# Sliding-window attention followed by a squared-ReLU MLP: six x tiles, margins on DMA landings, biases of the first blocks by TensorE, and the second block's loads on SyncE's queue

## The chip, the cores and the metric

One core of one Trainium2 chip. The metric is device time in microseconds (us) of that core, median over executions; one of them is taken with the hardware profiler. The profiled span is from the first to the last instruction and is 1.7 to 1.8 us shorter than the time that is measured from outside (before: 314.6 against 312.9).

## The reference, cut to what matters

```python
# q, k, v: [8 batches, 8 heads, 576 tokens, 64], float32
scores = scale * q @ k.T                      # per batch and head
rel    = pos[:, None] - pos[None, :]
mask   = (rel >= 0) & (rel < 128)             # window of 128 tokens
scores = where(mask, scores - slopes[h] * abs(rel), -1e9)
attn   = softmax(scores) @ v
x      = attn, heads side by side             # [4608 tokens, 512]
h      = x @ w_in                             # [4608, 2048]
out    = (maximum(h, 0) ** 2) @ w_out         # [4608, 512], float32
```

## The kernel before

The whole program is laid out by a list scheduler at build time: every piece of work is a task with engines, a cost, dependencies and buffers, and the plan is emitted in the order of its estimated starts. Each engine then works through its list in order and waits on semaphores. Some 60 hand-tuned adjustments (`ADJ`) shift single tasks.

The parts that matter here are the order of the first loads, the number of blocks whose keys and queries are loaded by the hardware queues (`N_HW`; the others are cast and loaded by GpSimd), and the buffers:

```python
FIRST = ["b0", "b1", "b2", "i0", "i1", "o0", "b3", "i2", "i3", "o1", "o2", "o3", "b4", "b5", "b6", "b7"]
N_HW = 1                 # b = block of 128 tokens (k, q, v), i = quarter of w_in, o = quarter of w_out
SIZE = {"kq": 4, "v": 9, "kqT": 7, "P": 3, "x": 3}
...
        if split:        # m < N_HW: float32 pieces into a stage, by SyncE and ScalarE, then a cast on chip
            stage = stages[m]
            ...
                        e.dma_start(view(stage, i)[:, r], source(src, m, split)[:, :, r])
        else:            # one cast-in-flight load each for keys and queries, by GpSimd
                    nc.gpsimd.dma_start(view(kq[s_kq[m].idx], i), source(src, m, split))
```

A block's keys and queries are transposed (by TensorE for the first eight blocks, by DMA transposes on SyncE's queue after them), 64-row matmuls give the scores, ScalarE the exponentials, and a product with a precomputed mask on VectorE brings in window and bias:

```python
                nc.scalar.activation(flat(Pt[sP.idx]), sS[i].tile..., AF.Exp, bias=0.0, scale=scale)
                ...
                    nc.vector.tensor_tensor(flat(Pt[sP.idx]), flat(Pt[sP.idx]), flat(masks), op=ALU.mult)
```

In the profile, `tp` are transposes of keys and queries, `s` scores, `P` probabilities, `pv` products with values, `x` the normalized attention, `xp` and `xT` its transposes, `h` products with w_in, `rt` their rectification, `g` the squares, `o` products with w_out.

The softmax here doesn't subtract the row's maximum and nothing guards it: scores larger than these inputs give would overflow.

Of the kernel before, what the change touches and what calls it, by code (L numbers as in the profile page):

```python
# [15 lines left out]
FIRST = ["b0", "b1", "b2", "i0", "i1", "o0", "b3", "i2", "i3", "o1", "o2", "o3", "b4", "b5", "b6", "b7"]  # L16
DIAG = [[0], [1], [2], [3], [4, 5], [6, 7]]
N_HW = 1
N_PE = 8
N_CUT = 1  # L20
N_PVH = 0
N_WARM = 8
FILL = 0.7
LEAD = 720
# [3 lines left out]
UNITS = {0: [(0, 128, 4), (128, 128, 4), (256, 128, 4), (384, 128, 4)], 1: [(0, 256, 2), (256, 256, 2)],  # L28
         2: [(0, 256, 2), (256, 256, 2)]}
PIECES = [4, 4, 4, 4]  # L30
CUT = 384
SIZE = {"kq": 4, "v": 9, "kqT": 7, "P": 3, "x": 3}
# [3 lines left out]
    "e1.2": 99737.5, "e14.1": 197.91, "e16.2": -128.81, "e19.2": -8999803.95, "e2.3": -401.4, "e20.1": 2.03,  # L36
    "e3.1": 99809.35, "e6.3": 99108.3, "fc3.1": -547.61, "fc3.2": -237.14, "fc3.3": -684.14, "fc3.5": -652.43,
    "fc3.7": -100007.3, "fc3.8": -9000379.3, "m18.2": 165.47, "m18.3": -239.22, "n1.1": 100203.0, "n10.1": 495.17,
    "n12.1": 587.74, "n15.0": 308.11, "n16.0": 356.11, "n16.1": 706.81, "n9.0": 332.79, "o0.2.0": -103.48,
    "o0.2.1": -122.14, "o0.2.2": -99562.6, "o1.0.1": -100260.7, "o1.0.2": -100228.4, "o1.1.1": -99628.0,  # L40
    "o1.1.2": -152.7, "o1.1.3": -198.1, "o1.3.1": -99940.7, "o2.0.1": -99143.6, "o2.1.1": 200, "o2.2.0": -615.0,
    "oe1.0.0": -220.3, "ones2": 99179.7, "pv11.1": -99297.74, "pv19.0": -100068.55, "r18.0": 267.47, "r3.1": 99545.79,
    "relufc3.1": -100188.3, "relufc3.5": -99571.3, "reluu0.0.2": -99848.1, "reluu0.1.0": -100044.0,
    "reluu1.1.4": -579.61, "reluu2.0.5": -282.54, "squ0.0.0": -100027.7, "squ1.1.3": -388.31, "squ2.1.1": 40,
    "u0.2.0": -8999828.5, "u0.2.1": -99868.0, "u1.1.0": 39, "u1.1.1": -99305.4, "u1.1.4": -99991.3,
    "u1.1.6": -99367.7, "u2.0.5": -99873.0, "u2.0.6": -468.21, "u2.0.7": -99687.4, "u2.1.1": -187.45,
    "u2.1.2": -482.59, "u2.1.3": 39, "u2.1.7": -266.7,
# [3 lines left out]
class Task:  # L51
# [3 lines left out]
                 "ready", "start", "end", "eng", "seq", "lat", "dma", "name", "count", "gap")  # L55

    def __init__(self, engs, key, emit, deps=(), acq=(), rel=(), lat=None, dma=None, name="", count=1):
        self.engs, self.key, self.emit = engs, key, emit
        self.deps = [d for d in deps if d is not None]
        self.acq, self.rel, self.lat = list(acq), list(rel), lat  # L60
        self.dma, self.name, self.count = dma, name, count
        self.users, self.ready, self.start, self.end, self.eng, self.gap = [], 0.0, None, None, None, 0.0
# [9 lines left out]
class Plan:  # L72


    LAT = {"PE": 210.0, "ACT": 60.0, "DVE": 80.0, "POOL": 200.0, "SP": 200.0, "ACTQ": 200.0}
    BEGIN = {"POOL": 840.0, "SP": 740.0, "ACTQ": 740.0, "ACT": 2550.0, "DVE": 860.0, "PE": 1190.0}
# [4 lines left out]
    NEAR = {"PE": 25, "ACT": 60, "DVE": 25}  # L81
# [17 lines left out]
    def order(self):  # L99
# [16 lines left out]
        def avail(t):  # L116
            at = t.ready
            if t.dma is not None:
                lane = self.lanes["SW" if "POOL" in t.engs else "HW"]
                if len(lane) >= self.LANES:  # L120
                    at = max(at, lane[-self.LANES])
# [15 lines left out]
        while len(done) < n_all:  # L137
# [40 lines left out]
            for u in t.users:  # L178
                left[u] -= 1
                at = st + dur if u.engs.keys() == {e} and t.dma is None else t.end  # L180
                if "SP" in u.engs and t.dma is None:
                    at += self.TO_SP
                u.ready = max(u.ready, at)
# [9 lines left out]
def kernel(  # L193
# [44 lines left out]
    masks = const.tile([128, H, 2, 128], BF16)  # L238
    dist = const.tile([128, 2, 128], FP32)
# [35 lines left out]
    def act(n):  # L275
        return n * 0.95 + 115.0

    def dve(n, rate=1):
        return n / rate / 0.96 + 180.0

    def dve_p(n, rate=1):
        return n / rate / 0.96 + 185.0
# [31 lines left out]
    t_ident = plan.add({"DVE": 230.0}, EARLY + 1, build_ident, [t_iota], name="ident")  # L314
# [7 lines left out]
    for part in (1, 0):  # L322
        key = EARLY + 2 if part else -1e5 + 1100
        t_dist[part] = plan.add({"DVE": 430.0}, key, lambda part=part: build_dist(part), [t_ident],
                                name=f"dist{part}", later=0.0 if part else 18000.0)
        for p in range(H):
# [3 lines left out]
            t_mask[part].append(plan.add({"ACT": act(128)}, key + 1 + p, build_mask, [t_dist[part]], name=f"mask{part}.{p}"))  # L330

    def ones(ts):
        for t in ts:
            nc.vector.memset(t[:, :, D:D + 1], 1.0)
    t_ones = [plan.add({"DVE": 320.0}, EARLY + 3, lambda: ones(tiles["v0"][0:2]), name="ones0"),
              plan.add({"DVE": 900.0}, -1e5 + 300, lambda: ones(tiles["v0"][2:]), name="ones1", later=11000.0),
              plan.add({"DVE": 1200.0}, -1e5 + 900, lambda: ones(tiles["v"]), name="ones2", later=20000.0)]
# [4 lines left out]
    def zero():  # L342
        for m in halves:
            if m - B < size["v"]:
                nc.vector.memset(tiles["v"][m - B][64:128, :, 0:D], 0.0)
            if m - B < size["kqT"]:
                nc.vector.memset(tiles["kqT"][m - B][:, 0:C, 64:128], 0.0)
    t_zero = plan.add({"DVE": 1300.0}, -1e5 + 950, zero, name="zero", later=25000.0)


# [29 lines left out]
    def load_block(m, key):  # L380
# [10 lines left out]
        if split:  # L391
            stage = stages[m]
            t_l = []
            for i, src in enumerate((k, q)):
                for r, (eng, e) in enumerate((("SP", nc.sync), ("SP", nc.sync) if m else ("ACTQ", nc.scalar))):
                    def fetch(i=i, src=src, r=r, e=e):
                        e.dma_start(view(stage, i)[:, r], source(src, m, split)[:, :, r])
                    t_l.append(plan.add({eng: 740.0}, key + 0.1 * i, fetch, dma=330.0, lat=700.0 if i else 1650.0,
# [7 lines left out]
            engs = {"DVE": 480.0, "ACT": 600.0} if m else {"DVE": 480.0}  # L406
# [4 lines left out]
        else:  # L411
            def fetch_kq():
                for i, src in enumerate((k, q)):
                    nc.gpsimd.dma_start(view(kq[s_kq[m].idx], i), source(src, m, split))  # L414
            t_kq[m] = [plan.add({"POOL": 1780.0}, key, fetch_kq, [], [s_kq[m]], dma=2 * ns,
                                name=f"lkq{m}", count=2)]

        def fetch_v():
            nc.gpsimd.dma_start(tile_of(s_v[m])[0:n, :, 0:D], source(v, m))  # L419
        l_v = plan.add({"POOL": 890.0}, key + 0.2, fetch_v, [t_zero] if kb == HALF else [], [s_v[m]],  # L420
                       dma=ns, name=f"lv{m}")
        t_v[m] = [l_v, t_ones[0 if m < 2 else 1 if m < B else 2]]
# [26 lines left out]
    def transpose_kq(m, due):  # L449
# [4 lines left out]
        if m >= N_PE:  # L454
            def flip():
                nc.sync.dma_start_transpose(out=tile_of(sT)[:, :, 0:n], in_=kq[s_kq[m].idx][0:n, :])
            t_f = plan.add({"SP": 1500.0}, due - 60, flip, t_kq[m] + [t_zero if kb == HALF else None], [sT],
                           [s_kq[m]], dma=1700.0 * n / 128, name=f"kqT{m}")
            t_kqT[m] = [[t_f], [t_f]]
            return  # L460
        t_tp, evs = [None, None], [[], []]
        for i in range(2):
# [13 lines left out]
            pieces = [(0, C // 2), (C // 2, C)] if i and m == 0 else [(0, C)]  # L476
            for c0, c1 in pieces:
                def evac(i=i, st=st, c0=c0, c1=c1, e=len(evs[i])):
# [4 lines left out]
                    else:  # L483
# [4 lines left out]
                                       [t_tp[i]] + evs[i], [], [st], name=f"ev{m}.{i}.{c0}"))  # L488
        last["tp"] = t_tp[1]
        t_kqT[m] = [[evs[0][0], evs[1][0]], evs[0] + evs[1]]  # L490

    def job(j, kind, ms, due):
        nb = len(ms)
        n = 64 if kind == "half" else 128
        for m in ms:
            transpose_kq(m, due)
        before = {m: at[seq[m][0], seq[m][1] - 1] for m in ms if kind != "diag"}
# [15 lines left out]
        bursts = [[0], [1]] if j == 0 else [[0, 1]]  # L513
        for z, grps in enumerate(bursts):
# [15 lines left out]
            for m in set(ms) | set(before.values()):  # L530
                deps += t_kqT[m][0] if z == 0 and len(bursts) > 1 else t_kqT[m][1]
# [11 lines left out]
        for i in range(4):  # L543
# [12 lines left out]
            def mask(w=w, flat=flat):  # L556
                if kind == "full" or (kind == "diag" and nb == 1):
# [13 lines left out]

    def values(j, kind, i, m, nb, sP, t_P, mb, due):
# [4 lines left out]
        if kind == "full":  # L577
            parts = [(slice(0, 128), mb), (slice(128, 256), m)]
# [250 lines left out]
```

## Time and profile before

| | before |
|---|---|
| time, median of 4 runs | 314.64 us (314.49 to 315.82) |
| profiled span, granted TensorE clock | 312.9 us, 1.00 |
| first product with weights / first output product | 15.18 / 20.26 us |
| last store issued / landed / end of span | 310.24 / 311.81 / 312.90 us |

(When the prediction was made three runs were known, with a median of 314.77.)

The chain that ended last, followed back from the end (page of before, share of the span by engine):

```profile
PE 78%; DMA 16%; POOL 3%; issue 1%; ACT 0%; POOLq 0%; SPq 0%
```

and the same chain in order of time for the first 45 us (start us, us, what):

```profile
6.82 0.85 POOL vf L419
7.67 7.46 DMA w_in_sb<-in_moe_w_in_dram
15.14 0.28 issue
15.42 14.97 DMA w_out_sb<-in_moe_w_out_dram
30.39 0.28 issue
30.68 9.89 DMA vf<-in_v_dram
```

Up to 40 us nothing but DMAs of the GpSimd queue stands in it.

### The profile page before, as it was taken

The numbers are of one execution on the slowest core, as the hardware profiler recorded it, in microseconds if no ns is written. First come the engines' busy times: TensorE is split into PE (matmuls) and PEld (weight loads), VectorE is DVE, ScalarE is ACT, GpSimd is POOL, SyncE is SP. The second block draws the span as 40 slices with busy tenths as digits, with TensorE's granted clock in tenths as the row PEclk, the third lists the DMA queues.
The fourth block names the chain that finished last, engine by engine and source line by source line (L and its number), as shares of the span: only waits on it lengthen the run. The fifth ranks groups of instructions, "written<-read, shape, count | busy, mean of one in ns | idle before, by whom it ended". The sixth has DMA issues, their size and how long they took to land.

```text
span 312.9 us, 7112 instructions
## 1 busy us (share of the span) xinstructions
PE 302.9 (97%) x2777; PEld 175.3 (56%) x2820; DVE 171.1 (55%) x492; ACT 173.2 (55%) x336; POOL 105.6 (34%) x131
## 2 busy tenths in 40 slices
PE   6899999999999999999999999999999999999996
PEld 3779757677766744455545554545454444444443
DVE  3757366667666656776666657666656222222211
ACT  4766567657677535855766554676564443444400
POOL 8844597272623855401937203700000000000000
DMA  9999999999999999997999939991220100010022
GB/s 130 184 192 204 172 176 183 144 153 147 206 133 190 198 158 192 145 124 137 152 183 173 180 60 130 197 175 52 51 69 17 69 34 35 37 34 34 34 96 74
DMA packets 165714, 39.54 MB, mean 126 GB/s; under 512 B 156336, under 2 KB 161200, under 8 KB 165680
## 3 DMA queue, kind: packets, MB, share of 16 engines
q0 software_dynamic: 114656, 18.10, 83.8%
q1 hardware_dynamic: 50592, 20.65, 35.8%
q8 instruction: 22, 0.36, 0.4%
q10 hardware_dynamic: 432, 0.33, 0.4%
q14 instruction: 12, 0.10, 0.1%
HBM read 36.70 MB, written 9.44 MB: 147 GB/s over the span
## 4 chain that ended last, share of the span: by engine, by line
PE 78%; DMA 16%; POOL 3%; issue 1%; ACT 0%; POOLq 0%; SPq 0%
PE o L762 34%; PE h L735 27%; PE h L718 7%; PE pv L593 5%; PE s L526 5%; DMA w_out_sb<-in_moe_w_out_dram 5%; DMA kqT<-kq 3%; DMA vf<-in_v_dram 3%; DMA kq<-in_q_dram 3%; DMA w_in_sb<-in_moe_w_in_dram 2%; POOL kq L414 2%; POOL vf L419 1%; POOL vt L419 0%; POOL dist L305 0%; ACT osb L291 0%
## 5 line engine op out<-in xcount | busy, mean ns | idle before, releaser
L762 PE MATMUL o<-w_out_sb,g 128*128 128x512 bf16 (+2 forms) x565 | 138.4, 373 | 1.9 <-DMA w_out_sb<-in_moe_w_out_dram 0.3
L683 ACT ACTIVATE rt<-h 128x512 bf16<-128x512 f32 x144 | 85.5, 606 | 92.0 <-PE h L735 64.1
L692 DVE TENSOR_TENSOR g<-rt 128x512 bf16<-128x512 bf16 x144 | 59.9, 422 | 74.0 <-ACT rt L683 73.3
L735 PE MATMUL h<-xT,w_in_sb 128*128 128x512 bf16 x368 | 95.1, 379 | 0.8
L762 PEld LDWEIGHTS <-g 128*128 128x128 bf16 x592 | 54.1, 98 | 56.0 <-issue 0.4
L550 ACT ACTIVATE P<-s 128x512 bf16<-128x512 f32 (+1 forms) x136 | 67.3, 581 | 18.1 <-PE s L526 18.1
L735 PEld LDWEIGHTS <-w_in_sb 128*128 128x128 bf16 x384 | 35.3, 98 | 39.5
L558 DVE TENSOR_TENSOR P<-P,masks 128x512 bf16<-128x512 bf16 (+1 forms) x112 | 44.4, 404 | 15.7 <-ACT P L550 11.2
L718 PE MATMUL h<-xT,w_in_sb 128*128 128x128 bf16 (+1 forms) x512 | 46.7, 246 | 1.3 <-DMA w_in_sb<-in_moe_w_in_dram 1.3
L414 POOL DMA_DIRECT2D kq<-in_k_dram x39 | 33.4, 857 | 40.3 <-DMA kqT<-kq 32.5
L718 PEld LDWEIGHTS <-w_in_sb 128*128 128x128 bf16 x512 | 38.4, 98 | 6.6 <-DMA w_in_sb<-in_moe_w_in_dram 1.6
L419 POOL DMA_DIRECT2D vt<-in_v_dram x32 | 27.0, 847 | 43.6 <-PE pv L593 35.4
L615 DVE TENSOR_TENSOR x<-pv,rec 128x256 bf16<-128x256 f32 (+1 forms) x80 | 33.4, 421 | 3.9 <-DMA xT<-x 1.5
L414 POOL DMA_DIRECT2D kq<-in_q_dram x39 | 33.6, 861 | 4.6 <-PE h L718 1.6
L593 PEld LDWEIGHTS <-P 128*128 128x128 bf16 (+1 forms) x576 | 25.1, 101 | 13.0 <-DVE x L615 1.3
L291 ACT ACTIVATE osb<-o 128x512 f32<-128x512 f32 (+1 forms) x23 | 13.6, 592 | 21.0 <-PE o L762 20.8
L611 DVE RECIPROCAL rec<-pv 128x4 f32<-128x4 f32 (+1 forms) x80 | 14.0, 178 | 18.7 <-PE pv L593 17.0
L593 PE MATMUL pv<-vt,P 128*128 128x65 bf16 (+1 forms) x448 | 23.8, 194 | 0.0
L526 PEld LDWEIGHTS <-kqT 64*128 64x128 bf16 x448 | 12.4, 94 | 8.1 <-issue 7.4
L289 DVE COPY osb<-o 128x512 f32<-128x512 f32 (+1 forms) x14 | 9.5, 682 | 13.2 <-PE o L762 12.6
L526 PE MATMUL s<-kqT 64*128 64x128 bf16 (+1 forms) x256 | 15.6, 210 | 0.0
L526 PE MATMUL s<-kqT,kqT 64*128 64x128 bf16 (+1 forms) x192 | 11.4, 209 | 0.2 <-DMA kqT<-kq 0.2
(41 smaller groups left out, 98.2 us busy)
## 6 DMA issues: line engine op xcount, KB each, us to landing
out_dram<-osb SPq DMA_DIRECT2D x31, 256.0 KB, 3.6
kq<-in_k_dram POOLq DMA_DIRECT2D x31, 128.0 KB, 7.1
kq<-in_q_dram POOLq DMA_DIRECT2D x31, 128.0 KB, 7.3
vt<-in_v_dram POOLq DMA_DIRECT2D x24, 128.0 KB, 8.2
w_in_sb<-in_moe_w_in_dram POOLq DMA_DIRECT2D x4, 512.0 KB, 11.1
w_out_sb<-in_moe_w_out_dram POOLq DMA_DIRECT2D x4, 512.0 KB, 15.0
vf<-in_v_dram POOLq DMA_DIRECT2D x8, 128.0 KB, 6.6
out_dram<-osb SPq DMA_DIRECT2D x8, 128.0 KB, 2.3
```

The lines of the kernel that those rows point to most:

```text
L414: nc.gpsimd.dma_start(view(kq[s_kq[m].idx], i), source(src, m, split))
L419: nc.gpsimd.dma_start(tile_of(s_v[m])[0:n, :, 0:D], source(v, m))
L526: nc.tensor.matmul(sS[2 * g2 + r].tile[:, jj * 256 + c0:jj * 256 + c0 + w], tile_of(s_kqT[mk])[rows, c, :], tile_of(s_kqT[mq])[rows, C + c ...
L550: nc.scalar.activation(flat(Pt[sP.idx]), sS[i].tile.rearrange("p (j t) -> p j t", j=2)[:, :, lo:hi], AF.Exp, bias=0.0, scale=scale)
L558: nc.vector.tensor_tensor(flat(Pt[sP.idx]), flat(Pt[sP.idx]), flat(masks), op=ALU.mult)
L593: nc.tensor.matmul(sv.tile[0:n, hi * (D + 1):(hi + 1) * (D + 1)], Pt[sP.idx][:, place(h)].rearrange("p t q -> p (t q)")[:, w], tile_of(s_v ...
L615: nc.vector.tensor_tensor(xt[sx.idx][0:n, hf * 256:(hf + 1) * 256].rearrange("p (h e) -> p h e", h=4), heads(sv)[0:n, :, 0:D], sr.tile[0:n ...
L683: nc.scalar.activation(srt.tile[:, 0:n], slot.tile[:, 0:n], AF.Relu, bias=0.0, scale=1.0)
L692: nc.vector.tensor_tensor(o, i, i, op=ALU.mult)
L718: nc.tensor.matmul(slot.tile[:, f * w:(f + 1) * w], w_in_sb[:, cc, fc * 128:(fc + 1) * 128], xT[:, cc, lo:lo + w], start=cc == 0, stop=cc ...
L735: nc.tensor.matmul(slot.tile, w_in_sb[:, cc, fc * 128:(fc + 1) * 128], xT[:, cc, g * 512:(g + 1) * 512], start=cc == 0, stop=cc == C - 1)
L762: nc.tensor.matmul(slot.tile[:, 0:hi - lo], gt[:, fc, t * 128:(t + 1) * 128], w_out_sb[:, fc, lo:hi], start=fc == 0, stop=fc == FCB - 1)
```

## The change

Its intent: start the products with weights sooner by taking the second block's keys and queries off the GpSimd queue; take the masks of the four first blocks off VectorE by letting TensorE add the bias to the scores; and let the plan assume later DMA landings than estimated (`SLACK`, in ns), with more x tiles to allow for it, so that TensorE's list in the middle of the run does not meet a transfer that is still under way. The core of the diff (the new adjustments, new cost estimates of single instructions and bookkeeping are cut; cut too is that the exponentials which build the masks, no longer needed by the first four blocks, are planned after 14 us):

```diff
-FIRST = ["b0", "b1", "b2", "i0", "i1", "o0", "b3", "i2", "i3", "o1", "o2", "o3", "b4", "b5", "b6", "b7"]
+FIRST = ["b0", "b1", "b2", "i0", "i1", "o0", "b3", "i2", "o1", "o2", "i3", "b4", "o3", "b5", "b6", "b7"]
-N_HW = 1
+N_HW = 2
+SLACK = {"kq": 0.0, "kqT": 5000.0, "v": 4000.0, "x": 2000.0}
-LEAD = 720
+LEAD = 320
-SIZE = {"kq": 4, "v": 9, "kqT": 7, "P": 3, "x": 3}
+SIZE = {"kq": 4, "v": 8, "kqT": 7, "P": 3, "x": 6}
...
+                at += t.slack
                 u.ready = max(u.ready, at)
...
+    def lone(j, m, due):
+        sS = [Slot("a") for _ in range(2)]
+        def biases():
+            for r in range(2):
+                nc.tensor.matmul(bank(sS[r], f"s{r}"), ident,
+                                 slopes[:, 4 * r:4 * r + 4].rearrange("p c q -> p (c q)"), start=True, stop=False)
...
+                    nc.tensor.matmul(sS[r].tile[:, c * 128:(c + 1) * 128], tile_of(s_kqT[m])[rows, c, :],
+                                     tile_of(s_kqT[m])[rows, C + c, :], start=False, stop=c == C - 1)
...
+                nc.scalar.activation(lone_P(sP)[:, r * 512:(r + 1) * 512], sS[r].tile, AF.Exp, bias=0.0, scale=scale)
```

## The prediction

> **What bounds the kernel now.** I read the page first, then the chain of waits, then TensorE's own timeline, then four-microsecond windows of the start, and last each DMA's issue and landing in the trace.
>
> ```profile
> span 312.9 us, 7112 instructions
> PE 302.9 (97%) x2777; PEld 175.3 (56%) x2820; DVE 171.1 (55%) x492; ACT 173.2 (55%) x336; POOL 105.6 (34%) x131
> ...
> PE   6899999999999999999999999999999999999996
> ...
> DMA  9999999999999999997999939991220100010022
> ```
>
> TensorE is full from the third slice (16 us) to the last; VectorE and ScalarE are just over half busy. Matmul busy time hides pipelining, so I also counted. The built program has 2820 matmuls. At the start-to-start pitch that full runs show (215 ns for 512 columns, 109 for 256, 55 for 128, 29 for 65, and 28 for each of a pair of 64-row score matmuls) they need 290.0 us, 5.9 of it warm-up and filler products that compute nothing. Real work is 284.1 us, and 312.9 - 284.1 = 28.8 us are lost. By start-to-start times, run by run, about 14.3 lie before 20.3 us (5.9 filler, 8.4 waiting), about 11.3 between 20.3 and 305, and 3.2 after the last matmul has started (evacuation and store).
>
> The 11.3 are almost no waiting: each of the 32 bursts of 64-row score matmuls costs about 0.10 us on entry and 0.12 on leaving (7 us together), and the rest is 0.01 to 0.04 at each change of operand. The change keeps these bursts. So only the first 20 us can give anything.
>
> ```profile
> 4.71 0.39 PE L270 MATMUL tp<-warm 128*128 128x128 bf16 x4
> 6.39 0.40 PE L470 MATMUL tp<-ident,kq 128*128 128x128 bf16 x4 [1.29 <-DVE kq L289]
> ...
> 13.96 0.28 PE L593 MATMUL pv<-vf,P 128*128 128x65 bf16 x4 [0.28 <-ACT P L550]
> 15.18 1.07 PE L718 MATMUL h<-xT,w_in_sb 128*128 128x128 bf16 x16 [0.94 <-DMA w_in_sb<-in_moe_w_in_dram]
> ...
> 17.76 1.96 PE L718 MATMUL h<-xT,w_in_sb 128*128 128x128 bf16 x32 [0.39 <-DMA w_in_sb<-in_moe_w_in_dram]
> ...
> 20.26 1.02 PE L762 MATMUL o<-w_out_sb,g 128*128 128x512 bf16 x3 [0.32 <-DMA w_out_sb<-in_moe_w_out_dram]
> ```
>
> These are lines of TensorE's timeline (start, duration, what, idle before it and who ended it). The reader should see that the first product with weights (15.18), the next (17.76) and the first output product (20.26) start as their weights land: 15.14, 17.71, 20.22 in the trace. From there the DMA stream, in order on the GpSimd queue, stays just ahead of TensorE: a block's keys and queries land at 38.90 and 39.73, and that block's transposes run here:
>
> ```profile
> 38.00 1.89 PE L762 MATMUL o<-w_out_sb,g 128*128 128x512 bf16 x8
> 39.72 0.61 PE L470 MATMUL tp<-ident,kq 128*128 128x128 bf16 x8
> ```
>
> No idle time stands before it, but there is no room either. That is why TensorE cannot simply run two microseconds further ahead.
>
> **What the Trainium skill says.** (1) "TensorE: Matmul & The Clock Gate", section "Wait — 56ns, not 53.3ns?": warm matmuls start N / 2.4 GHz + about 2.5 ns apart, cold ones N / 1.2 GHz. The trace agrees: 16 products of 128 columns take 0.90 us, the first eight warm-up products start 427 ns apart. (2) "DMA: Bandwidth & Descriptors", section "Issuing engines are not separate DMA queues": DMAs from all issuers share 16 engines, and a second issuer saves only issue time. The trace of before fits: while ScalarE's and SyncE's loads still run, the GpSimd queue moves 421 packets in the fifth microsecond, against some 1200 per microsecond afterwards. (3) The same page, section "Specifications": below 512 B a transfer is off line rate. Keys, queries and values come in 256 B pieces, a 128 KB load takes 0.84 us of the stream, while a 512 KB load of weights takes 2.55. (4) "PSUM — Partial Sum Buffer", section "The four PSUM rules": a matmul without the first-flag adds to what the bank holds, which is what the bias products rely on. No run yet shows it.
>
> **The change, part by part.** *Biases by TensorE.* For the four lone first blocks, slopes times distance is put in the bank by eight 512-column products with the identity: 8 x 0.215 = 1.72 us more TensorE work. It removes 16 mask products on VectorE (289 ns each) and turns 16 exponentials of 256 columns (388 ns) into 8 of 512 (606 ns): at the back-to-back pitch of about 0.27 and 0.5 us ScalarE gains nothing, VectorE is freed of about 4.5 us that nobody waits for after 16 us. Three of the four pairs fall in the wait before the first weights, the fourth (0.43) at its edge. One score burst less is split, saving about 0.4 us of transitions in the same stretch. Net work to be placed before the block at 39.7 us: +1.3 us.
>
> *Second block by SyncE.* Its two loads leave the GpSimd queue, so the first quarter of w_in becomes the sixth instead of the eighth load there: issue at 7.67 - 2 x 0.87 = 5.93 us. If only the issue counted, everything behind would land 2 x 0.84 = 1.7 us sooner. But the same bytes go over the same engines, in larger pieces and written as fp32. I estimate some 1.2 us of stream time for them (the first block's four such loads are in flight from about 2 to 5.8 us, sharing). So the stream comes 0.5 to 1.2 us sooner; I take 0.8. New on the way are two casts (the first block's two take 542 ns on average), for a block that is not first in line.
>
> *w_in by quarters* is nominal: pieces of four rows of columns stand in both kernels. What changes is the order: i2, o1, o2, i3, b4, o3, in place of i2, i3, o1, o2, o3, b4. The same number of loads stands before b5.
>
> *Six x tiles, eight v tiles, margins.* In the middle of the run they let the score bursts sit up to 5 us later than the transposes' landing and finish attention earlier. The one visible wait of this kind before is 0.20 us (scores of block 9, on a landing at 62.57). I count 0.3 us.
>
> *Sum.* Walk the new order of TensorE with these durations: the first weights land at about 14.3, where blocks 0 to 2 are nearly done; the second unit follows at 16, and it is dense from there. TensorE alone could then reach the transposes of block 5 with about 10.3 us lost (start, filler, waits) instead of 13.5, counted with the burst transitions as work in both. The stream allows less: queries of that block land at 39.73 - 0.8 = 38.9 and the work ahead of their transpose is now 27.7 us, so at least 11.2 us are lost. Gain 13.5 - 11.2 = 2.3, less the 1.3 of added work = 1.0, plus 0.3 from the middle: 1.3 us. The end is untouched. 314.8 - 1.3 = 313.5 us.
>
> **The rivals.** *The stream is not faster at all* (its engines were full from 5 us on, not issue-bound). For it: landings before are 0.84 us apart while issues are 0.87 apart, and the slices read 9 from the start. Then the gain is 1.0 - 0.8 + 0.3, about 0.5 us: 314.3. *The issue was the bound*: the stream comes 1.7 us sooner, TensorE's own order limits, gain about 2.2: 312.6. For it: in the first slice the core moves 130 GB/s, in the next three 184 to 204. *A new wait at the start*: the transposes of block 1 now stand ahead of block 0's scores; if its keys, third on SyncE's queue, land after 8 us, block 0 moves back about a microsecond, and block 2 with it, past the landing of the weights. Then 0.5 to 1 us is lost: 314.5 to 315. *ScalarE becomes the bound in the middle*: attention is packed tighter, two blocks in about 9 us, some 16 exponentials and five rectifications of 0.5 us, about 6.5 of 9 us. Against it: it is under 80%, but bursts of four exponentials can hold back a rectification and with it one of two banks; 32 such waits of 0.1 us would cost 3 us: 316.5.
>
> **Range and chances.** Most paths lie between 312.3 and 315; I allow for a gain in the middle that I can't see and for the rectification wait: 311.5 to 315.4. Faster by over 2% needs under 308.5, which would ask for 6 of the 8.4 us of waiting at the start with nothing given back to the biases; 0.03. Slower by over 2% (321.1) needs a repeated new wait in the middle; 0.02.
>
> **What would show it.** Right: the first weights product between 13.5 and 14.7 us; TensorE without gaps over 0.3 us from 17 us; transposes of block 5 at about 38.7 to 39; lost time before 20 us near 12 in place of 14.3, with 1.7 us in the new bias line; the middle still at about 11 us. Wrong: first weights at 15 or later (stream bound), or at 13.3 with TensorE not ready; idle time of TensorE on rectifications or xT after 100 us; a middle that loses under 9 us, which would mean that transitions I call fixed were waits.

## The result, and the profile after

| | before | after |
|---|---|---|
| time, median of 4 runs | 314.64 us (314.49 to 315.82) | 314.88 us (314.87 to 314.95) |
| ratio, 95% interval | | 1.000 (0.9976 to 1.0024): same |
| profiled span, clock | 312.9 us, 1.00 | 313.1 us, 1.00 |
| first weights / first output product | 15.18 / 20.26 us | 14.91 / 20.80 us |
| last store issued / landed / end | 310.24 / 311.81 / 312.90 us | 309.81 / 311.41 / 313.12 us |

All runs are fast. A ratio is the mean time of one kernel's fast runs over that of the other's in the same rounds, so it is not quite the ratio of the medians. The result is correct, so the scores do add to what the bias products leave in the bank: the prediction's fourth point from the skill holds.

The page of after, the lines that answer to those of before:

```profile
span 313.1 us, 7099 instructions
PE 305.5 (98%) x2793; PEld 174.1 (56%) x2793; DVE 168.8 (54%) x492; ACT 167.9 (54%) x320; POOL 103.6 (33%) x129
...
PE   8789999999999999999999999999999999999995
...
DMA  9999999999999999998999999962111000010122
...
PE 94%; DMA 2%; SPq 1%; ACT 1%; DVE 1%; issue 0%; DVEq 0%
```

The sums have hardly moved, but the last line has: DMAs make up 2% of the chain in place of 16%. Its pieces in order of time (chain of after, first 45 us):

```profile
3.63 0.60 SPq L431
4.27 5.72 DMA stage<-in_q_dram
10.09 0.91 DVE kq L297
10.99 0.10 DVE rec L685
11.11 0.43 DVE x L694
...
14.88 1.07 ACT P L633 x2
15.95 0.79 ACT masks L337 x4
16.74 0.50 ACT rt L762
17.28 1.07 PE h L798 x16
18.37 0.61 ACT rt L762
19.02 1.95 PE h L798 x32
```

This is the moved load. SyncE issues its loads some 0.65 us apart. Block 1's last piece of queries is issued at 4.27 and lands at 9.99, VectorE casts it (0.91 us), and only then normalizes block 0 (`rec`, `x`). From there the chain runs through the transposes and scores of the next blocks to two exponentials and four mask exponentials on ScalarE, and then the first rectification. TensorE's own timeline shows what that does (start, duration, what, idle before):

```profile
8.73 0.40 PE L505 MATMUL tp<-ident,kq 128*128 128x128 bf16 x4 [0.72 <-ACT kq L299]
...
14.91 1.06 PE L798 MATMUL h<-xT,w_in_sb 128*128 128x128 bf16 x16
...
17.28 1.05 PE L798 MATMUL h<-xT,w_in_sb 128*128 128x128 bf16 x16 [0.41 <-ACT rt L762]
...
19.02 1.95 PE L798 MATMUL h<-xT,w_in_sb 128*128 128x128 bf16 x32 [0.46 <-ACT rt L762]
20.80 1.03 PE L842 MATMUL o<-w_out_sb,g 128*128 128x512 bf16 x4
```

The first quarter of w_in lands at 13.92, 1.22 us sooner than before, and waits there for a whole microsecond until TensorE takes it at 14.91. The first output product's weights land at 19.44 and are taken at 20.80. From 22 to 300 us no wait of TensorE above 0.2 us is left.

The landings of the GpSimd stream in the two traces (us):

```
            w_in 0   w_in 1   w_out 0   block 3 k / q     block 5 k / q
before      15.14    17.71    20.22     21.08 / 21.92     38.90 / 39.73
after       13.92    16.46    19.44     20.29 / 21.12     38.73 / 39.56
sooner by    1.22     1.25     0.78      0.79 / 0.80       0.17 / 0.17
```

The lead of 1.2 us has shrunk to 0.17 by the block at which the prediction draws its balance.

And hardly any of the 1.2 us is the change's. Block 2's values, the last load before the first quarter of w_in, land at 11.32 in before and at 11.38 in after. A load reports its landing in 16 steps (the semaphore records of the traces): of the first quarter of w_in, 15 steps stand by 13.78 us in before and by 13.77 in after. Only the last step differs, 15.14 against 13.92. Two experiments below, b_lane0 and b_lane7, run the plan of before with nothing changed until the last stores, and there the quarter lands at 14.18 and 14.23. So before's 15.14 is a late step of one execution. What stands beside it is a 16 KB transfer of an instruction queue from 14.03 to 15.00 us. Every one of the 14 traces has one such transfer of 0.95 to 0.98 us; it starts between 14.0 and 16.4 us, and in seven traces the last step of the load in flight comes 0.9 to 1.4 us after the 15th. In after it starts at 15.72, past that landing. It does not explain every late step (in e_hw1 the quarter's last step is 0.66 us behind, and the transfer starts only at 14.77), and no run moves it, so the cause is not shown.

In b_lane7 TensorE was not held by that load at all: it landed at 14.23 and was taken at 14.75, after ScalarE:

```profile
14.63 0.28 PE L593 MATMUL pv<-vf,P 128*128 128x65 bf16 x4 [0.28 <-ACT P L550]
14.75 1.06 PE L718 MATMUL h<-xT,w_in_sb 128*128 128x128 bf16 x16
```

The transposes of block 5 in after:

```profile
38.69 1.03 PE L842 MATMUL o<-w_out_sb,g 128*128 128x512 bf16 x4
39.55 0.61 PE L505 MATMUL tp<-ident,kq 128*128 128x128 bf16 x8
```

39.55 in place of 39.72, with no wait before it.

**The end.** The last store of before and that of after, in the timelines (ACTq is ScalarE's queue):

```profile
310.24 0.35 ACTq L786 DMA_DIRECT2D out_dram<-osb  x1
```

```profile
309.81 0.36 ACTq L866 DMA_DIRECT2D out_dram<-osb  x1
```

The changed kernel issues its last store 0.43 us *earlier*, and still its span ends 0.22 us *later*. From the landing of that store to the end are 311.81 to 312.90, 1.09 us, in before and 311.41 to 313.12, 1.71 us, in after. The trace of the sequencers, which keep their own records, shows what stands there (after, start us, engine, what):

```
311.43 SyncE   wait for the semaphore of the last store (first of eight, in fixed order)
311.49 ... 311.86   seven more waits, 0.06 us apart, all long fulfilled
311.92, 311.99 two drains
312.02 GpSimd  semaphore instruction
312.40 GpSimd  the next one (0.38 us later; in before it is 0.08)
312.49 ... 313.10   drains, semaphores cleared, end
```

SyncE's closing list waits for the eight semaphores that the hardware DMAs use in turn. Before issues 109 such DMAs, so the last store signals the fifth and three waits follow it. After issues 113, so it signals the first and seven follow. Of the 0.62 us more, four waits of 0.06 us make 0.25, the two GpSimd instructions stand 0.30 further apart, and the drains after them take 0.07 more.

**The sum, as the prediction counted it** (lost time is the excess of TensorE's start-to-start times over the pitches given there; up to 40 us with the warm-up and filler products, and a split score burst less booked under work):

| term | predicted | two traces |
|---|---|---|
| lost time at the start | -2.3 | 13.62 to 11.74, less the 0.4 of the burst: -1.5 |
| added work | +1.3 | +1.3 (booked, not its cost: see the price of the bias products) |
| middle (40 to 300 us) | -0.3 | 10.8 to 10.55: -0.26 |
| end | 0 | 3.19 to 3.85: +0.66 |
| sum | -1.3 | +0.2 |

### The profile page after: what moved, and what is told of

Same layout as the page of the kernel before. It is cut to its first block, busy times and chain, and to the rows that moved or that the text cites. A ratio compares the mean times of both kernels' runs of the same rounds, so it can differ in the third digit from the quotient of the medians.

```text
span 313.1 us, 7099 instructions
## 1 busy us (share of the span) xinstructions
PE 305.5 (98%) x2793; PEld 174.1 (56%) x2793; DVE 168.8 (54%) x492; ACT 167.9 (54%) x320; POOL 103.6 (33%) x129
## 4 chain that ended last, share of the span: by engine, by line
PE 94%; DMA 2%; SPq 1%; ACT 1%; DVE 1%; issue 0%; DVEq 0%
PE o L842 40%; PE h L815 27%; PE h L798 14%; PE pv L668 6%; PE s L564 5%; DMA stage<-in_q_dram 2%; SPq L431 1%; PE tp L505 1%; PE xp L714 0%; PE s L625 0%; ACT rt L762 0%; ACT P L633 0%; DVE kq L297 0%; ACT masks L337 0%; PE s L616 0%
## 5 line engine op out<-in xcount | busy, mean ns | idle before, releaser
L842 PE MATMUL o<-w_out_sb,g 128*128 128x512 bf16 (+2 forms) x592 | 141.7, 373 | 0.0
L815 PE MATMUL h<-xT,w_in_sb 128*128 128x512 bf16 x384 | 96.6, 379 | 0.0
L588 ACT ACTIVATE P<-s 128x512 bf16<-128x512 f32 x120 | 62.4, 607 | 8.5 <-PE s L564 8.4
L596 DVE TENSOR_TENSOR P<-P,masks 128x512 bf16<-128x512 bf16 x96 | 39.9, 421 | 13.5 <-ACT P L588 9.7
L694 DVE TENSOR_TENSOR x<-pv,rec 128x256 bf16<-128x256 f32 (+1 forms) x80 | 31.3, 414 | 0.7
L668 PEld LDWEIGHTS <-P 128*128 128x128 bf16 (+1 forms) x576 | 23.1, 101 | 9.1 <-DVE P L596 0.8
L297 DVE COPY osb<-o 128x512 f32<-128x512 f32 (+1 forms) x18 | 12.3, 684 | 17.2 <-PE o L842 17.1
L668 PE MATMUL pv<-vt,P 128*128 128x65 bf16 (+1 forms) x448 | 21.4, 194 | 0.0
L299 ACT ACTIVATE osb<-o 128x512 f32<-128x512 f32 (+1 forms) x19 | 11.0, 580 | 18.3 <-PE o L842 18.3
L685 DVE RECIPROCAL rec<-pv 128x4 f32<-128x4 f32 (+1 forms) x80 | 11.4, 167 | 5.6 <-PE pv L668 4.7
```

The source lines that it names most:

```text
L588: nc.scalar.activation(flat(Pt[sP.idx]), sS[i].tile.rearrange("p (j t) -> p j t", j=2)[:, :, lo:hi], AF.Exp, bias=0.0, scale=scale)
L668: nc.tensor.matmul(sv.tile[0:n, hi * (D + 1):(hi + 1) * (D + 1)], prob, tile_of(s_v[mk])[:, h, 0:D + 1], start=mk == parts[0][1], stop=mk ...
L694: nc.vector.tensor_tensor(o, heads(sv)[0:n, :, 0:D], sr.tile[0:n, :].unsqueeze(2).to_broadcast([n, 4, D]), op=ALU.mult)
L815: nc.tensor.matmul(slot.tile, w_in_sb[:, cc, fc * 128:(fc + 1) * 128], xT[:, cc, g * 512:(g + 1) * 512], start=cc == 0, stop=cc == C - 1)
L842: nc.tensor.matmul(slot.tile[:, 0:hi - lo], gt[:, fc, t * 128:(t + 1) * 128], w_out_sb[:, fc, lo:hi], start=fc == 0, stop=fc == FCB - 1)
```

## The experiments

Twelve kernels ran, in four calls of the same number of rounds (five); the runs of one call share a chip and the runs of before. Median of before: 314.66, 314.93, 314.66, 314.49, each with 11 runs that scatter from 314.0 to 315.8. No experiment is beyond that scatter unless it is said; so most readings below rest on single steps in the traces, and not on the whole time. These steps scatter too. In seven traces the start is one of the two plans, and only late stores and a last GpSimd instruction differ (us):

| trace | plan of the start | first weights landed / taken | block 5's transposes | last store issued |
|---|---|---|---|---|
| before | before | 15.14 / 15.18 | 39.72 | 310.24 |
| b_lane0 | before | 14.18 / 15.85 | 39.84 | 310.09 |
| b_lane7 | before | 14.23 / 14.75 | 39.72 | 310.00 |
| after | after | 13.92 / 14.91 | 39.55 | 309.81 |
| c_after | after | 14.15 / 14.97 | 39.61 | 310.21 |
| e_end | after | 13.70 / 14.44 | 39.10 | 309.44 |
| e_pool1 | after | 14.29 / 15.13 | 39.77 | 311.00 |

(In b_lane0 TensorE waited 2.00 us up to 7.06, and its clock was halved from 7.64 to 11.05, so its first products ran late.) A difference of a few tenths of a microsecond between two traces is therefore not an effect of an edit by itself. The 0.43 us by which after's last store leads before's is of this size: the means over these traces are 310.11 for the plan of before and 310.12 for that of after.

### Where the last store's semaphore stands in the closing list

Three kernels change only this, by cutting late output stores into halves of 64 rows, which adds hardware DMAs:

```diff
 # e_end: after, seven stores cut, 120 hardware DMAs.  b_lane0: before, four cut, 113.  b_lane7: before, three cut, 112
+                w = 64 if n == 128 and (g, t) in CUT_STORES else n
-                (nc.scalar if final else nc.sync).dma_start(
-                    out[b * S + kb * 128:b * S + kb * 128 + n, lo:hi], so.tile[i * 64:i * 64 + n, 0:hi - lo])
+                for r0 in range(0, n, w):
+                    (nc.scalar if final else nc.sync).dma_start(
+                        out[b * S + kb * 128 + r0:b * S + kb * 128 + r0 + w, lo:hi],
+                        so.tile[i * 64 + r0:i * 64 + r0 + w, 0:hi - lo])
```

> The changed kernel with seven of its late output stores (128 rows) cut in two stores of 64 rows, so that seven more DMAs go over the SyncE queue and the last store of the program lands on the eighth of the eight hardware-DMA semaphores instead of the first. Theory END: the program's closing list waits for the eight semaphores in a fixed order at about 0.06 us each; in the changed kernel the last store's semaphore comes first, so seven waits follow its landing (in the kernel before it is the fifth, three follow). With it last the run is 7 x 0.06 = 0.4 us shorter: 314.5 us, and from the last store's landing to the end of the span about 1.3 us instead of 1.7. Rival: the 1.7 us in the trace were chance; then 314.9.

> The kernel before with four of its late output stores cut into two halves of 64 rows. All work and its order stay; the number of hardware DMAs becomes 113 as in the changed kernel, so that the last store signals the first of the eight semaphores that SyncE's closing list waits for, in place of the fifth. END theory: four more waits of 0.06 us follow the last landing, so 1.09 us from landing to end become about 1.34, and the time rises by 0.25 us to 314.9. If the other 0.3 us that the changed kernel shows there also hangs on the semaphore's place, 1.7 us and +0.6. Rival (the closing list has no part in it): 1.09 us and the time of before, within 0.1.

> The kernel before with three of its late output stores cut in halves: 112 hardware DMAs, so that the last store signals the last of the eight semaphores. END theory: no wait follows, the stretch from landing to end shrinks from 1.09 to about 0.9 us and the time falls by 0.18 us against before, and by 0.43 against the run with four stores cut. Rival: no difference to before or to the run with four stores cut beyond 0.1 us.

A fourth adds a single GpSimd instruction to the first:

```diff
 # e_pool1: e_end, and
+    spare = const.tile([128, 1], FP32)
...
         for t in done:
             t.emit()
+        nc.gpsimd.memset(spare, 0.0)
```

> The changed kernel with seven late output stores cut in halves (last store on the last semaphore, as in the run tried first) and one instruction more at the end of GpSimd's program: a memset of one unused column. In all seven traces where GpSimd's program left 202 records, its two closing semaphore instructions are 0.38 us apart and an 8 KB fetch stands in the last 0.1 us; in the five traces with 203 or 204 records they are 0.08 apart and there is no such fetch. FETCH theory (the closing list is delayed where the program's length makes GpSimd fetch its last instructions then): 203 records, 0.08 us apart, 0.93 us from the last landing to the end in place of 1.29, and 314.2 us, some 0.4 to 0.5 under before. Rival (the delay comes from something else in the changed kernel): 0.38 apart, 1.29 us, 314.5.

(Of the traces kept here, the counts of seven and five were six and four at that time; e_bias2 and e_slack0 with 202 records have the gap as well.) Measured in the traces (last column from the landing of the last store to the end of the span):

| kernel | its semaphore | GpSimd records | closing GpSimd pair apart | landing to end |
|---|---|---|---|---|
| before | fifth | 203 | 0.08 | 1.09 |
| b_lane0 | first | 203 | 0.08 | 1.35 |
| b_lane7 | eighth | 203 | 0.08 | 0.93 |
| after | first | 202 | 0.38 | 1.71 |
| e_end | eighth | 202 | 0.39 | 1.29 |
| e_pool1 | eighth | 203 | 0.08 | 0.91 |

Both terms add: first to eighth place is 0.42 us in either kernel (1.35 - 0.93 and 1.71 - 1.29), and one GpSimd instruction more takes away 0.38 us (1.29 - 0.91). With both, the changed kernel closes 0.80 us faster than it did. In the run with tiles and margins undone (below) GpSimd has 201 records, and there the gap of 0.39 us stands one instruction later in the closing list, at the drain. So it goes with the length of GpSimd's program, in all traces kept. That it is a fetch of instructions is a guess: an 8 KB transfer of an instruction queue stands at the very end of the traces with the gap and is missing in those without it, but it starts after the gap and is no proof.

The whole times are too coarse to confirm 0.2 to 0.4 us: e_end 314.53 us (ratio 0.9996, 0.998 to 1.0012), b_lane0 314.87 (1.0019, 0.998 to 1.0057) and b_lane7 314.65 (0.9993, 0.9971 to 1.0016), against 314.66 for before in the first call and 314.93 in the second. e_pool1 did not get its 314.2 but 315.01 (1.0005). Its profiled execution lost the gain, and more, in the middle, in a wait that the changed kernel's first trace does not have (e_pool1, then after; TensorE's timeline):

```profile
81.96 2.79 PE L799 MATMUL h<-xT,w_in_sb 128*128 128x256 bf16 x24 [0.80 <-DMA xT<-x]
```

```profile
80.79 2.78 PE L798 MATMUL h<-xT,w_in_sb 128*128 128x256 bf16 x24
```

The DMA transpose of x into xT lands at 81.91 in the one and 80.58 in the other. The transfer itself takes about as long in both (5.74 and 5.59 us); it is issued later, at 76.18 and 74.99, although x is complete at 71.17 and 70.95. Before it in SyncE's list stands the transpose of another block's keys and queries, and that waits for queries on the GpSimd stream, which land at 73.49 and 72.13. SyncE's longest waits from 60 to 78 us (after, then e_pool1; total, times, longest):

```profile
SPq L491 <- DMA kq<-in_q_dram: 10.6, 4, 4.5
SPq L492 <- DMA kq<-in_q_dram: 10.1, 3, 6.1
```

So a late load holds up an x that has long been ready, because one queue serves both in order. No run changes that order.

### The stream: second block back on the GpSimd queue

> A control, the changed kernel itself, for comparison on one chip with the three that follow. Expected: 314.9 us within 0.3, some 0.2 us over before; the first weights product at 14.9, block 5's transposes at 39.5, and 1.7 us from the last landing to the end. If it comes out below before, the difference of 0.2 us between the two kernels is noise of the chip or of the placement of the program and nothing is to be explained.

```diff
 # e_hw1: after, with four stores cut as above (so that the last store's semaphore is after's, the first)
-N_HW = 2
+N_HW = 1
```

> The changed kernel with the second block's keys and queries back on the GpSimd queue as before (four stores cut in halves, so that the last store signals the same semaphore as in the changed kernel). STREAM theory (the engines are shared, so where a load is issued hardly matters): the first quarter of w_in lands about 1.2 us later than the changed kernel's 13.92, near 15.1, but block 5's queries land within 0.3 us of 39.56, and the time stays within 0.3 us of the control. The prediction's view (0.8 us gained for the whole stream): queries at about 40.4 and the time 0.5 to 0.8 us over the control.

| | c_after (control) | e_hw1 |
|---|---|---|
| time | 315.21 us (314.81 to 315.28) | 315.13 us (315.05 to 316.96) |
| ratio to before | 1.0006 (0.9987 to 1.0024) | 1.0014 (0.999 to 1.0039) |
| w_in quarter 0 landed / taken | 14.15 / 14.97 | 14.73 / 14.78 |
| w_out quarter 0 landed / taken | 19.68 / 20.86 | 19.91 / 19.95 |
| block 5 queries landed / transposes start (keys first) | 39.38 / 39.61 | 39.42 / 39.22 |

The plan is made anew, so this is not the two loads alone: GpSimd's program has 204 records, and the closing gap is 0.08 us, so from the last landing to the end it is 1.34 us in place of the control's 1.70. Equal whole times so contain 0.36 us gained at the end and about as much lost elsewhere.

The queries land within 0.04 us of the control's. So the two loads may be issued on either queue: it changes when a byte is moved, not how many bytes are moved by 39 us. The control's lead of 0.6 us at w_in bought nothing in the last row: with the loads *undone*, TensorE takes each weight as it lands and reaches block 5's transposes 0.39 us earlier than the control. That fits a start that no longer hangs on SyncE's loads and their casts, but 39.22 lies within the scatter of the changed plan (39.10 to 39.77), so it is no proof. A wait of 0.69 us on the same xT transpose at 81 us follows.

### The chain to the first weights

If the cast and the order around it hold TensorE, taking them off the chain should help. e_start casts block 1's queries on ScalarE and moves four tasks; e_start_tp5 also moves two output products around block 5's transposes:

```diff
 # e_start, applied to the finished plan of after: what, and after which task
+    move("b1", ["tp0.1"])
+    move("tp1.0", ["s0"])
+    move("ev1.0.0", ["tp1.0", "one0.7"])
+    move("cq1", ["e0.1"])          # and its engine becomes ScalarE
 # e_start_tp5, besides
+    move("o0.1.3", ["o0.0.3", "squ0.1.3"])
+    move("s4", ["o0.2.0"])
```

> The changed kernel with its planned order kept, but with block 1's bias products and block 0's scores ahead of the transposes of block 1's keys, and the cast of block 1's queries on ScalarE (idle there) instead of VectorE. Theory START: the 1 us between the landing of the first weights (13.9) and their first use (14.9) is the order's own; with it mended everything behind comes 0.9 us sooner, so 314.0. Theory STREAM: the first weights' product does start at about 14.0, but the queries of block 5 land at 39.6 whatever TensorE does, and its transposes stood at 39.8 already; TensorE waits there some 0.7 us, and the run gains 0.2 at most: 314.7.

> The same as e_start, and besides two output products of 0.86 us that are ready are put ahead of block 5's transposes and of the scores of blocks 4 and 5. Theory STREAM: with other work at the place where the landing holds TensorE up, the 0.9 us from the start survive: 314.0. Theory START: no more than e_start gives, since nothing was held there. If neither gains, the start is not worth what I think.

e_start: first weights at 14.58 in place of 14.91, block 5's transposes at 39.21 in place of 39.55, and this third of a microsecond stays to the last store (309.47 against 309.81). But this is the fastest of its six executions, and e_end, whose start is after's unchanged, has 14.44, 39.10 and 309.44: the gain is not told from scatter. Block 5's queries landed at 39.25 here, and their part of the transposes ran at 39.43, close behind. e_start_tp5: first weights at 14.09, 0.22 us after they land, earlier than in any trace of the changed start, but then it loses 0.55 us on block 3's queries, 0.46 on a square and 0.37 before products with values (by start-to-start times; the profile's idle times there are 0.37, 0.28 and 0.18); its last store is at 310.16, later than after's. In the whole time neither gains: 315.35 us (1.0017, 0.9999 to 1.0035) and 315.46 us (1.0026, 1.001 to 1.0042; this one is measurably slower than before). So at block 5 TensorE's chain stands some 0.2 us behind the stream (the queries' transposes at 39.77 and their landing at 39.56 in after); that a chain freed alone runs into the stream is seen once, in e_start_tp5's wait on block 3's queries. A rival stays untested: after, e_start and e_start_tp5 have the same two waits, of 0.41 and 0.46 us, on rectifications before the second and third product with weights, and in after the first rectification stands on ScalarE behind the mask exponentials that the change moved there. No run moves these away.

### The price of the bias products

e_nobias leaves them out, which makes the result WRONG (relative error 0.51); e_bias2 does them twice, with a correct result:

```diff
 # e_nobias: after
-                nc.tensor.matmul(bank(sS[r], f"s{r}"), ident, slopes[...], start=True, stop=False)
+                bank(sS[r], f"s{r}")           # and the first score matmul of each bank starts it
 # e_bias2: after
+            for r, stop in ((0, True), (1, True), (0, False), (1, False)):
+                nc.tensor.matmul(sS[r].tile, ident, slopes[...], start=True, stop=stop)
```

> The changed kernel without the eight bias products (the result is wrong on purpose: no mask and no bias on the first blocks), in the same order, with the same exponentials. My prediction booked them as 1.3 us of added work that ate most of the gain; if so, it returns 1.0 to 1.7 us: 313.2 to 313.9. Theory STREAM: three pairs stand in waits and the rest is given back at block 5's landing: 314.6 or above.

> The changed kernel with the eight bias products of the four lone blocks done twice: 1.72 us more TensorE work before 17 us and nothing else; the result stays correct. If the start is held by landings and by the chain to the first blocks, as the run without the bias products suggested, the added products fall into waits and the time stays within 0.4 us of 315. If each microsecond of added work costs one, as the prediction's sum counted it, 316.6 us, and the first weights product moves from 14.9 to about 16.

e_bias2: 315.88 us (1.0031, 1.0015 to 1.0048), 1.22 over before, where the changed kernel was 0.24 over it: so 1.72 us of added products cost 1.0 us. In the trace the first weights move from 14.91 to 15.90 and block 5's transposes from 39.55 to 40.54, by 0.99 both; the other 0.7 falls into waits such as the 0.72 us before block 1's transposes. Neither theory of this run was right: the truth is between.

e_nobias: its six executions fall into two groups, 314.81 to 314.88 us at a mean clock of 0.999 to 1.0, and 316.61 to 317.04 at 0.989. The profiled one is of the second group (windows view; the columns after the length are busy us of PE, PEld, DVE, ACT, POOL, then granted clock, DMA share, GB/s):

```profile
8.00:12.00 4.00, 2.07 (x34) 1.37 (x32) 1.95 (x7) 1.72 (x3) 3.34 (x5) 0.94 1.82 196
12.00:16.00 4.00, 3.85 (x42) 2.91 (x43) 2.41 (x6) 2.46 (x7) 1.64 (x3) 0.50 1.24 206
16.00:20.00 4.00, 3.33 (x44) 3.21 (x43) 2.38 (x10) 2.81 (x9) 0.74 (x1) 0.71 1.72 184
```

Without the bias products TensorE is busy for half of the stretch from 8 to 12 us, and then its clock is halved. In the executions that keep the clock the time is the changed kernel's 314.88, so taking away 1.72 us of work returned nothing. The bias products are work in a gap, and with them the clock stayed up here. The kernel before, which has none, shows a mean clock of 0.993 to 0.995 in 13 of its 44 executions; the ten of the changed kernel are all at 0.999 or 1.0.

### Tiles and margins

```diff
 # e_slack0: after
-SLACK = {"kq": 0.0, "kqT": 5000.0, "v": 4000.0, "x": 2000.0}
+SLACK = {"kq": 0.0, "kqT": 0.0, "v": 0.0, "x": 0.0}
 # e_middle0: the same, and
-SIZE = {"kq": 4, "v": 8, "kqT": 7, "P": 3, "x": 6}
+SIZE = {"kq": 4, "v": 9, "kqT": 7, "P": 3, "x": 3}
```

> The changed kernel with three x tiles and nine v tiles as before, and all margins on DMA landings at 0; the plan is made anew from that (its hand-tuned adjustments stay those of the changed kernel). Prediction's view: the middle (20 to 300 us) loses 0.3 us more than the changed kernel's 11.2, so 315.1 to 315.3. Rival (the margins and tiles are what holds TensorE's middle together): single waits of 0.2 to 1 us on DMA landings appear, 1 to 3 us more in the middle, 316 to 318. Rival (they do nothing): within 0.1 us of the control's 315.2 less what the start scatters.

> The changed kernel with its six x tiles and eight v tiles, but all margins on DMA landings at 0 (the plan is made anew; the same number of hardware DMAs, so the same closing list). It splits the run that undid tiles and margins together (319.1 us, one wait of 2.53 us on an xT landing, 4.4 us over before). MARGIN theory: the margins are what keeps TensorE off the landings; the wait on xT at about 79 us comes back with 1 to 2.5 us and the time is 316.5 to 319. TILE theory (three x tiles hold back the transposes to xT): with six tiles no wait over 0.3 us appears, and the time is 314.9 to 315.4. In between: both have a part.

These are the only experiments with a large effect: e_middle0 319.07 us (1.0133, 1.0108 to 1.0157), e_slack0 318.49 us (1.0111, 1.0078 to 1.0144). Both have the same wait in the same place. e_middle0:

```profile
78.76 2.78 PE L798 MATMUL h<-xT,w_in_sb 128*128 128x256 bf16 x24 [2.53 <-DMA xT<-x]
```

e_slack0, timeline and windows:

```profile
78.58 4.45 PE L798 MATMUL h<-xT,w_in_sb 128*128 128x256 bf16 x24 [2.38 <-DMA xT<-x]
```

```profile
72.00:78.50 6.50, 4.14 (x53) 2.84 (x52) 3.80 (x14) 3.10 (x7) 3.97 (x6) 1.00 1.73 161
78.50:84.00 5.50, 5.42 (x45) 4.02 (x46) 1.16 (x3) 2.13 (x4) 3.96 (x6) 0.69 1.93 201
```

Six x tiles do not prevent it, so it is the margins. Without them the plan puts TensorE at the third group of tokens at about 76 us, with x transposes issued at 67.98 and 70.14 that take 8.2 and 8.3 us and land at 76.13 and 78.45. In e_slack0 the wait costs twice: the clock falls to 0.69 in the next stretch, and the same 24 products take 4.45 us in place of 2.78. In e_middle0's profiled execution a wait of about the same length left the clock alone; the executions of both kernels, 316.4 to 319.9 us, are as scattered as that suggests. One reservation: the hand-tuned adjustments were made with the margins in place, so the experiments show what the margins are worth inside this plan. The kernel before has a plan without margins and without such a wait; it was tuned in another way.

## Why the prediction was right or wrong

The class (within 2%) and the range (311.5 to 315.4) were right, and so was the reading that TensorE's middle holds almost nothing to gain. That only the first 20 us can give anything was not: the last microsecond differs by up to 0.80 us (after against e_pool1). The forecast of 1.3 us less was wrong in sign: it came out 0.2 us more, which is not told apart from nothing.

**The stream (0.5 to 1.2 us sooner, taken as 0.8).** This step failed where it mattered. The lead was 1.22 us at the first quarter of w_in and 0.17 us at block 5's queries, where the balance was drawn: the queries landed at 39.56 and not at 38.9. The argument that the bytes cross the same engines was right and should have been carried to its end. Bytes that are only moved to another queue returned no stream time here: e_hw1 shows 0.04 us between the two ways at 39 us, and even at the first quarter of w_in 15 of 16 steps stand at 13.78 and 13.77. The 1.22 us is one late step in before's trace, and b_lane0 and b_lane7 lack it; so the prediction's reading that the start of before waits for its weights (15.18 at 15.14) was a reading of that execution too. It was the first rival's case, which said 314.3; with the 0.66 us of the end that is 314.96, and 314.88 was measured. So close a fit of two small terms is partly luck.

**First weights between 13.5 and 14.7 us.** They landed in that range (13.92) and were taken at 14.91, the case that the prediction listed as wrong, "TensorE not ready". The chain shows why: block 1's queries, last on SyncE's queue, land at 9.99, and VectorE's cast of 0.91 us stands ahead of block 0's normalization. The third rival named this kind of wait, with keys landing after 8 us as its condition. They landed at 7.96, so the wait it described (0.72 us) came from the cast, and the longer chain came from the queries, which it did not consider.

**Lost time at the start, 13.5 to 11.2.** It fell to about 11.7 by the traces' sums, and 0.4 of that is the burst. This is the two points above in one number. Before 20 us, counted anew with the transitions of score bursts left out, lost time with fillers went from 13.2 (7.25 + 5.9) to 11.5 (7.56 + 3.98): all of the gain is fewer fillers; the waiting itself did not shrink.

**Added work, +1.3.** As work it is there; as a cost it is not confirmed. Doubled, the products cost 1.0 of 1.72 us, but taken away they returned nothing (e_nobias at full clock), which was not foreseen. That this follows from the stream's standing so near is argued, not shown.

**The middle, -0.3.** It measured -0.26 in the first pair of traces. But this is luck of a landing, on both sides: from block 5's transposes to the last product it is 269.96 us in before and 269.70 in after, but 269.69 and 269.72 in b_lane0 and b_lane7, the plan of before. And in the control the wait on xT at 81 us is 0.16 us and in e_hw1 and e_pool1 0.69 and 0.80, with the same plan there or nearly the same. That "one visible wait of 0.20 us" was all that margins could save was the wrong measure of them; inside the new plan they hold off a wait of 2.4 us.

**The end, untouched.** Wrong, +0.66 us, and the largest single miss: four more store DMAs turned the last one's semaphore from fifth to first in the closing list (+0.26 by b_lane0), and what goes with the length of GpSimd's program brought 0.38 us more (e_pool1). The last store itself is 0.43 us earlier in this pair of traces; over the seven traces of the two plans there is no difference. The ratios of the whole times, 1.000 and 1.0006 with an end that is 0.6 us longer, leave room for a gain of 0.4 to 0.6 us by all the rest; the intervals reach 0.6 to 0.75 us to either side, so it is not shown.

**ScalarE as the bound of the middle** (the fourth rival) did not occur: after 22 us no wait above 0.2 us is left in after's first trace.

**A better version.** None beats both kernels by more than the scatter. The nearest are e_end and b_lane7, with ratios of 0.9996 and 0.9993. The parts that the traces favour (second block back on the GpSimd queue, which by itself brings the short closing gap, and the last store on the eighth semaphore) were not run together. Why b_lane0 and b_lane7, which share their plan, land the first weights 0.05 us apart and the second quarter 0.78 us apart is only narrowed down: in b_lane0 the last of 16 steps comes 0.99 us after the 15th, in b_lane7 0.18, with the 16 KB instruction transfer at 15.63 and 14.70 us. What causes the scatter of landings stays open.

## What to carry to other kernels

Where loads run a fraction of a microsecond ahead of the engine that needs them, issuing some of them elsewhere gains nothing by itself: compare the *landing* at the point where the consumer will stand, and count what the moved load makes others wait for. Read the last microsecond of the trace as closely as the first; a term that "the change does not touch" can still move with the number of DMAs and instructions. And a plan with zero margin on DMA landings is priced by its worst landing, sometimes twice, because a wait can also cost the clock (2.38 us in e_slack0 did, 2.53 in e_middle0 did not). Before a lead seen in one pair of traces is explained, look whether a second execution of the same plan has it.

## What the Trainium skill lacked or had wrong

- "TensorE: Matmul & The Clock Gate", section "What's actually happening", gives the cold state "after ≥1 idle window (~3.4µs)". Here the clock was halved with less: for 3.4 us after a wait of 2.38 us (e_slack0) and after one of 2.00 us (b_lane0), and for 6.8 us with no single wait above 1.24 us, only sparse work (2.07 us busy of 4, e_nobias). A wait of 2.53 us in e_middle0 did not lower it. Elsewhere the page tells of throttling by frequent short idles, without a length. As a condition, a window without work is too strict, and the outcome is not the same from one execution to the next.
- "Runtime: NRT & Kernel Launch", section "The ~15µs preamble/postamble breakdown", gives some 1.5 us to a closing barrier of the runtime that waits for all engines. The closing list here is the program's own (its instructions carry the kernel's line), so it is another stretch, and no page that was read has it: 0.91 to 1.79 us between the last landing and the end. It varies with the place of the last store's semaphore in SyncE's list (0.06 us for each wait that follows, 0.42 from first to eighth) and goes with the number of GpSimd instructions (0.38 us from 202 to 203 records).
- "DMA: Bandwidth & Descriptors", section "Issuing engines are not separate DMA queues": the runs agree, with 0.04 us between two loads on one queue or the other (block 5's queries, e_hw1 against the control). What the page lacks is the scatter: the same load of the same plan landed at 16.46 and at 17.64 us in two executions (second quarter of w_in, after and c_after), most of the difference being in the last of its 16 steps (0.15 and 0.94 us after the 15th).
- No page that was read has a figure for what a 16 KB transfer of an instruction queue does to loads in flight: it takes 0.95 to 0.98 us in each trace's start, and in seven of 14 a last step is 0.9 to 1.4 us late beside it.
- "TensorEngine Tiling (Array Packing)" names a drain when the tiling mode changes but gives no time for it: between 128-row and 64-row matmuls 0.10 us are lost on the way in and 0.12 on the way out, in both kernels.
